# A second level of Strassen for three of the seven second-layer products, with their results added by an accumulating DMA

## The chip, the cores and the metric

The kernel runs on one core of a Trainium2 chip. The metric is the device time of one execution, in microseconds (us), as the median of several runs.

## The reference

A retention block feeds a feed-forward block. For each of 4 batches and 8 heads a state of 64 x 64 is carried over 768 positions, and its output is the input of two matrix products with a leaky ReLU between them:

```python
for t in range(S):
    state = gamma * state + einsum('bhd,bhe->bhde', k[:, :, t], v[:, :, t])
    y[:, :, t] = scale * einsum('bhd,bhde->bhe', q[:, :, t], state)
x = y.transpose(0, 2, 1, 3).reshape(B * S, H * D)     # 3072 tokens x 512
h = x @ w_in                                          # 512 x 2048
g = maximum(0.01 * h, h)
out = g @ w_out                                       # 2048 x 512
```

The weights come as float64 and are turned into float32 on the chip; all products are in float32.

## The kernel before

**Tiles.** The tokens are cut into six chunks c of 128 positions x 4 batches = 512 tokens. Activations lie with features on the partitions: x, g and o are tiles of 128 partitions x 4 blocks x 2 halves x 256 tokens. The hidden dimension is cut into four units u of 512. For each chunk and unit, the first layer multiplies a 512 x 512 piece of w_in by x, the leaky ReLU follows, and the second layer multiplies a 512 x 512 piece of w_out by g and adds the result to o.

**Strassen.** A 512 x 512 x 512 product is made by the Winograd form of Strassen: seven products M1 to M7 of 256-blocks from sums of blocks (`differences`, line 623, makes those of g in the tile gd and in g[1]). One such product is four matmuls of 128 x 128 weights by 256 columns (`seven`, line 641; its matmul is line 662). For chunks 2 to 5 the first layer goes one level further: each of its seven products is again made of seven products of 128-blocks, 49 in all. `inner` (line 1171) computes them in two groups, group 0 with 28 matmuls (M1, M4, M5 and M6 of the outer level) and group 1 with 21 (line 1184, 128 columns each); ScalarE and VectorE bring each bank to a tile `made`, and `outer` (line 1210) combines the seven results on VectorE (lines 1229 to 1239) and applies the leaky ReLU on ScalarE (line 1226). The weight sums for this are made once, kept in DRAM (`kept`), and streamed for each unit into the tiles wa and wb (`load_unit`, line 1054).

**The second layer** (`output`, line 735) takes seven products in the order FUSED: M1, M5, M6, M2, M7, M3, M4. Four PSUM rooms A, B, C, D (banks 5, 4, 7, 6) collect them: A holds M1 and then M1 + M2; ScalarE copies A to B after M1, so that B holds M1 + M6 and then also M7; C holds M5, then M5 + M3; D gets a copy of B and then M4. Each room is added to its block of o by VectorE (`plus`, line 606), or copied by ScalarE in the first unit of a chunk.

**Order.** The scheduling is manual: each engine does its instructions in the order in which the code writes them, and waits on semaphores only for data and for free buffers. The loop at line 1281 runs over 16 steps n, with c = 2 + n // 4 and u = n % 4. A step writes, in this order: the differences of g of unit n; group 0 of the first layer of unit n + 1; for u < 2 (and while a next chunk exists) a "visit", `joint_visit` (line 412), which reads the retention state for two batches of chunk c + 1 through banks 0, 1, 2 and 7; the second-layer products M1, M5, M6 of unit n; the scores of the next pair (`scores_of_pair`, line 356); M2; sums of the next x on VectorE (`differences` of x for u = 1, `sums_of_x` for u = 2); group 1 of the first layer of unit n + 1; M7; `outer`; M3 and M4. Banks 0 to 3 serve `inner`. In a visit, two memsets on GpSimd (`rows_free`, line 406) order groups of matmuls, and GpSimd then multiplies the next values by their decay (`decay_v`, line 158; its operation is line 161). All DMAs of this part are issued from SyncE (SP), one after another.

**Other names.** `new_g` (line 803) makes the tiles g and gd of a unit; `block(k, i)` (line 85) gives weight block i of half-unit k, where an even k = 2u belongs to the first layer and an odd one, 2u + 1, to the second; blocks 0 to 3 are the quarters, 4 to 6 the Strassen sums. `piece` (line 510) says where a loaded piece of weights goes. The line numbers are those of the kernel before.

## Time and profile before

| | us |
|---|---|
| median of three runs | 637.8 (637.6 to 638.4) |
| the profiled execution | 637.82 |
| its span, first to last instruction | 636.0 |
| TensorE busy in the span | 628.8 |
| VectorE busy | 464.1 |
| ScalarE busy | 268.9 |
| GpSimd busy | 23.3 |
| DMA: moved in all | 113.42 MB, 178 GB/s |

How to read it: the profile takes one execution. A group of instructions is one line of code, engine and operation with the tiles that it writes and reads, its count, its busy time and the mean duration of one, then the idle time of the engine ahead of it and what ended that. The fp32 matmul appears as two records. A duration in a group includes a part that overlaps with the next instruction, so that the distance from start to start is shorter. In the timelines, the first number is the start, the second the time until the last of the merged instructions ends; what stands in square brackets is the idle time before it and what released it. The chain of waits follows the execution back from its last instruction.

The stretches of the profile: chunks 0 and 1 up to about 224 us, the passage into the loop up to 252, then unit n = 0 (252 to 277), n = 1 to 3 (to 351), chunk 3 (n = 4 to 7, to 452), chunk 4 (n = 8 to 11, to 551), chunk 5 (n = 12 to 15).

### The profile page before, as it was taken

Reading aid. Unit: us, or ns where it says so; the run is one execution under the profiler, and the core shown is the slowest. Engines: PE = TensorE matmul, PEld = TensorE weight load, DVE = VectorE, ACT = ScalarE, POOL = GpSimd, SP = SyncE. Lnnn points to the kernel's source line nnn. Section 1 sums busy time; section 2 is a strip of 40 time slices with the busy share of each in tenths; the row PEclk is TensorE's granted clock in tenths of the full one; section 3 lists DMA queues with packets and bytes.
Section 4 is the critical chain, followed back from the end, with each engine's and each line's share of the span. In section 5 each row is a group of like instructions: output and inputs, shape, how many; then the busy total and the mean of one; then the engine's idle time right before and its main releaser. Section 6 shows DMA issues by size and latency. Waiting matters only on the chain.

```text
span 636.0 us, 14285 instructions
## 1 busy us (share of the span) xinstructions
PE 628.8 (99%) x6086; PEld 568.8 (89%) x6086; DVE 464.1 (73%) x760; ACT 268.9 (42%) x515; POOL 23.3 (4%) x45
## 2 busy tenths in 40 slices
PE   8999999999999999999999999999999999999997
PEld 5888888888888889899999999999999999999996
DVE  5679769889979986576785666877737768636655
ACT  4876556347343124242352442423433423534421
POOL 2000000000011010101000101000010000000000
PEclk9999999999999999999999999999999999999999
DMA  8941426556863998376735392864455236444201
GB/s 331 404 131 38 128 67 220 148 174 194 283 250 110 351 333 280 103 238 193 259 88 184 120 295 79 268 195 140 137 169 185 87 123 197 154 162 158 87 1 68
DMA packets 87537, 113.42 MB, mean 178 GB/s; under 512 B 3241, under 2 KB 71721, under 8 KB 87473
## 3 DMA queue, kind: packets, MB, share of 16 engines
q1 hardware_dynamic: 87168, 111.88, 53.2%
q8 instruction: 48, 0.79, 0.5%
q10 hardware_dynamic: 304, 0.62, 0.3%
q14 instruction: 17, 0.13, 0.1%
HBM read 93.35 MB, written 19.14 MB: 177 GB/s over the span
## 4 chain that ended last, share of the span: by engine, by line
PE 95%; DVE 2%; ACT 1%; DMA 1%; issue 0%; DVEq 0%; ACTq 0%
PE bank L662 32%; PE bank L1184 27%; PE C_h L662 4%; PE B_o L662 4%; PE A_h L662 4%; PE C_o L662 4%; PE A_o L662 4%; PE B_h L662 4%; PE D_h L662 2%; PE D_o L662 2%; PE d L683 2%; PE bank L369 1%; PE bank L444 1%; PE bank L427 1%; PE bank L380 1%; DMA t<-decay_dram 1%
## 5 line engine op out<-in xcount | busy, mean ns | idle before, releaser
L606 DVE TENSOR_TENSOR made<-made,bank 128x512 f32<-128x512 f32 (+1 forms) x96 | 56.4, 618 | 55.9 <-PE bank L1184 51.5
L606 DVE TENSOR_TENSOR o<-o,bank 128x512 f32<-128x512 f32 (+2 forms) x91 | 58.5, 661 | 51.8 <-PE bank L662 31.2
L662 PE MATMUL bank<-g,w 128*128 128x256 f32 x384 | 89.9, 382 | 0.0
L662 PEld LDWEIGHTS bank<-g,w 128*128 128x128 f32 x384 | 70.7, 190 | 9.2
L1184 PEld LDWEIGHTS bank<-x,wb 128*128 128x128 f32 x672 | 77.6, 192 | 0.8
L1184 PE MATMUL bank<-x,wb 128*128 128x128 f32 x672 | 77.6, 275 | 0.0
L1184 PE MATMUL bank<-x,wa 128*128 128x128 f32 x512 | 67.7, 275 | 0.0
L662 PE MATMUL bank<-gd,w 128*128 128x256 f32 x288 | 66.1, 379 | 0.0
L1184 PEld LDWEIGHTS bank<-x,wa 128*128 128x128 f32 x512 | 63.5, 192 | 1.1 <-ACT made L1194 0.2
L662 PEld LDWEIGHTS bank<-gd,w 128*128 128x128 f32 x288 | 54.7, 190 | 7.4
L1184 PE MATMUL bank<-t,wa 128*128 128x128 f32 x384 | 53.3, 275 | 0.0
L1226 ACT ACTIVATE g<-g 128x512 f32<-128x512 f32 x64 | 39.3, 631 | 30.8 <-DVE g L606 30.8
L1184 PEld LDWEIGHTS bank<-t,wa 128*128 128x128 f32 x384 | 48.0, 192 | 0.0
L1188 ACT COPY bank<-bank 128x512 f32<-128x512 f32 (+1 forms) x32 | 16.7, 520 | 67.8 <-PE bank L1184 67.5
L606 DVE TENSOR_TENSOR g<-made 128x512 f32<-128x512 f32 x64 | 42.7, 688 | 1.2
L755 ACT COPY bank<-bank 128x512 f32<-128x512 f32 x17 | 9.7, 570 | 71.2 <-PE bank L662 71.1
L609 DVE TENSOR_TENSOR gd<-g,gd 128x512 f32<-128x512 f32 x48 | 33.2, 692 | 5.4 <-ACT g L1226 0.5
L776 ACT COPY bank<-bank 128x512 f32<-128x512 f32 x16 | 9.1, 570 | 46.4 <-PE bank L662 46.4
L662 PE MATMUL bank<-g,last 128*128 128x256 f32 x120 | 28.3, 380 | 0.0
L662 PE MATMUL bank<-gd,last 128*128 128x256 f32 (+1 forms) x124 | 27.5, 373 | 0.0
L662 PE MATMUL A_h<-x,w 128*128 128x256 f32 x112 | 26.6, 380 | 0.0
L662 PEld LDWEIGHTS bank<-gd,last 128*128 128x128 f32 x124 | 22.8, 190 | 3.2 <-DVE gd L609 0.3
(223 smaller groups left out, 1030.1 us busy)
## 6 DMA issues: line engine op xcount, KB each, us to landing
wa<-kept SPq DMA_DIRECT2D x16, 1344.0 KB, 7.2
raw<-in_weights_dram SPq DMA_DIRECT2D x31, 512.0 KB, 4.4
wb<-kept SPq DMA_DIRECT2D x16, 896.0 KB, 5.7
wa<-kept SPq DMA_DIRECT2D x16, 448.0 KB, 4.4
wb<-kept SPq DMA_DIRECT2D x16, 448.0 KB, 6.3
out_dram<-o SPq DMA_DIRECT2D x23, 256.0 KB, 3.1
kept<-w SPq DMA_DIRECT2D x12, 448.0 KB, 6.0
qk<-in_qk_dram SPq DMA_DIRECT2D x10, 512.0 KB, 8.0
```

Source lines behind the costliest of these rows:

```text
L369: nc.tensor.matmul(at[j][ts(h, 64), n, m, i], lhsT=x[ts(j, 64), 1, a, ts(h, 64)], rhs=x[ts(j, 64), 0, a, ts(h, 64)], start=(n == 0 and a = ...
L380: nc.tensor.matmul(sums[h][ts(j, 64), n, a], lhsT=key[ts(h, 64), 2 * a + j], rhs=val[ts(h, 64), 2 * a + j], start=(n == 0 and a == 0), sto ...
L427: mm = nc.tensor.matmul(at[n][j][ts(i, 64), m, ts(h, 64)], lhsT=by_half[h][ts(j, 64), n, a], rhs=x[ts(j, 64), 0, a, ts(h, 64)], start=(n = ...
L606: nc.vector.tensor_tensor(out=out, in0=a, in1=b, op=ALU.add)
L609: nc.vector.tensor_tensor(out=out, in0=a, in1=b, op=ALU.subtract)
L662: nc.tensor.matmul(to, lhsT=block(w, sa)[:, k, ts(i, 128)], rhs=rhs[:, k, a:z], start=(first and (i == 0 or split) and n == 0 and k == 0), ...
L683: nc.tensor.matmul(banks[r][:, i, :], lhsT=block(2 * u, r + 2 * kh)[:, k, ts(i, 128)], rhs=x[:, 2 * kh + th, k, :], start=(step == 0 and i ...
L755: nc.scalar.copy(out=bank_of("B"), in_=ps)
L776: nc.scalar.copy(out=bank_of("D"), in_=ps)
L1184: nc.tensor.matmul(ps[q][:, i], lhsT=w[:, j, i], rhs=part_of(moving[i], s), start=(i == 0 and m in ("M1", "M5", "M4")), stop=True, skip_gr ...
L1188: nc.scalar.copy(out=ps[3], in_=ps[0])
L1226: nc.scalar.activation(g[:, i], g[:, i], AF.Prelu, alpha=0.01)
```

## The change

For units n = 4 to 14 (`by_leaves`: chunks 3, 4 and 5 without the very last unit) the second layer is split. The *trunk* computes M1, M5, M6 and M7 as before, without M2, M3 and M4, and without the copy to room D. The *leaves* compute M2, M3 and M4 by a second level: seven products of 128-blocks each, 21 matmuls of 128 columns in place of 12 of 256. They run through banks 6, 7, 2 and 5 after the trunk and after group 1 of the first layer.

- Their weight sums are made in chunk 2 on VectorE (`sums_of_rows`; u = 0 and 1 in step n = 0, u = 2 in n = 2, u = 3 in n = 3), stored to DRAM by 7 DMAs a unit (10 for u = 3), and loaded again for each unit by three DMAs from SP (`load_rows`).
- The sums of their moving operands are made by four subtractions a unit on GpSimd (`leaf_sums`), in units with a visit between the visit's memsets and the decay.
- Their results go to SBUF (`leaf_results`) by five copies on ScalarE and three additions on VectorE a unit. For u = 0, 1, 2 one accumulating DMA from GpSimd adds them to o[:, 0:3]; for u = 3 three additions on VectorE do, each followed by its store.
- What the trunk's rooms mean is spread in another way: A goes to o[0], B after M6 to o[1], B after M7 to o[2] and o[3], C to o[1] and o[3].
- The leaky calls of `outer` are deferred and written between the leaves' products.
- g and gd are one tile, with gd in reverse order, so that the operands of M2, M3 and M4 lie side by side; the weight blocks of odd half-units are placed anew for the same reason. The tiles that these blocks filled serve as leaf weights and scratch from chunk 3 on.

```diff
...
 
+    PLACE = {3: 4, 6: 3, 4: 6}
+
     def block(k, i):
...
         if k < N_UNITS - 1:
-            return unit(k)[:, i]
+            return unit(k)[:, PLACE.get(i, i) if k % 2 else i]
         return units[k][i // 2][:, i % 2] if i < 6 else last_s4[:, 0]
...
 
-    def joint_visit(c, b, banks=None):
+    def joint_visit(c, b, banks=None, behind=None):
 
...
             heads.pop((c, b + n))
+        if behind is not None:
+            behind()
         if later is not None:
...
 
+    PLACES = slice(2, 5, 2)
+
     def piece(n):
...
         if k < N_UNITS - 1:
+            if k % 2 and h:
+                return unit(k)[:, PLACES, i, :]
             return unit(k)[:, 2 * h : 2 * h + 2, i, :]
...
     slot = [0]
+    last_three = {}
+
+    class Reversed:
+
+        def __init__(self, tile):
+            self.tile = tile
+
+        def __getitem__(self, at):
+            return self.tile[:, 6 - at[1]]
 
...
         slot[0] = 1 - i
-        g = work.tile([128, 4, 2, N], FP32, tag=f"g{i}", name=f"g_{c}_{u}")
-        gd = work.tile([128, 3, 2, N], FP32, tag=f"gd{i}", name=f"gd_{c}_{u}")
-        return u, g, gd
+        both = work.tile([128, 7, 2, N], FP32, tag=f"g{i}", name=f"g_{c}_{u}")
+        last_three[c, u] = both[:, 2:5]
+        return u, both[:, 0:4], Reversed(both)
 
...
 
-    streamed = []
+    streamed, streamed_flat = [], []
     N2 = (NC - 2) * NU
...
         streamed.append(flat[:, 0 : 21 * C].rearrange("p (j i n) -> p j i n", j=7, i=3))
+        streamed_flat.append(flat)
 
...
         return block[:, k, ts(t, C)]
+
+    leaf_kept = [dram.tile([128, 3, 7, C], FP32, name=f"leaf_kept_{u}") for u in range(NU)]
+
+    def flat_of(part):
+        return part.rearrange("p i k n -> p (i k n)")
+
+    def leaf_rooms():
+
+        free = [flat_of(unit(k)[:, 2:5]) for k in (1, 3, 5)]
+        spare = [x2_place[0][:, 21 * C :], streamed_flat[0][:, 21 * C :]]
+        more = [spare[i // 2][:, ds(i % 2 * 3 * C, 3 * C)] for i in range(4)]
+        return free, spare, [x.rearrange("p (q n) -> p q n", q=3) for x in more]
+
+    def rows_of(u):
+
+        if u < NU - 1:
+            return [((0, 3, 1), unit(2 * u + 1)[:, 2:5])]
+        return [((0, 3, 2), units[2 * u + 1][1]), ((1, 2, 1), last_s4)]
+
+    def sums_of_rows(u):
+
+        free, _, more = leaf_rooms()
+        if u == NU - 1:
+            more = more[0:2] + [x[:, 7 * C : 10 * C].rearrange("p (q n) -> p q n", q=3)
+                                for x in free[0:2]]
+        bases = [[] for _ in range(3)]
+        for at, blocks in rows_of(u):
+            which = slice(*at)
+            a11, a21, a12, a22 = (blocks[:, :, k, ts(m, C)] for k in range(2) for m in range(2))
+            r = [x[:, which] for x in more]
+            plus(r[0], a21, a22)
+            minus(r[1], r[0], a11)
+            minus(r[2], a12, r[1])
+            minus(r[3], a11, a21)
+            for base, a in zip(bases, (a11, a12, a22)):
+                base.append((which, a))
+
+        def keep():
+            for j, parts in enumerate(bases):
+                for which, a in parts:
+                    nc.sync.dma_start(out=leaf_kept[u][:, which, j], in_=a)
+            for j, r in enumerate(more):
+                nc.sync.dma_start(out=leaf_kept[u][:, :, 3 + j], in_=r)
+        return keep
+
+    def load_rows(n):
+
+        free, spare, _ = leaf_rooms()
+        leaf_weights[:] = [x[:, 0 : 7 * C].rearrange("p (j n) -> p j n", j=7)
+                           for x in (free[0], free[1], spare[1])]
+        for to, kept_rows in zip(leaf_weights, (leaf_kept[at_of(n)[1]][:, i] for i in range(3))):
+            nc.sync.dma_start(out=to, in_=kept_rows)
+
+    leaf_weights = []
+
+    def by_leaves(n):
+        return n >= NU and n < N2 - 1
+
+    def leaf_sums(n):
+
+        free, spare, _ = leaf_rooms()
+        made = [x.rearrange("p (q n) -> p q n", q=3)
+                for x in (free[0][:, 7 * C : 10 * C], free[1][:, 7 * C : 10 * C],
+                          spare[0][:, 0 : 3 * C])]
+        three = last_three[at_of(n)]
+        b11, b12, b21, b22 = (three[:, :, k, ts(h, C)] for k in range(2) for h in range(2))
+        for out, a, b in ((made[0], b12, b11), (made[1], b22, made[0]), (made[2], b21, made[1]),
+                          (b12, b22, b12)):
+            nc.gpsimd.tensor_tensor(out=out, in0=a, in1=b, op=ALU.subtract)
+        return [b11, b21, *made, b22, b12]
+
+    def leaf_steps(n, moving):
+
+        ps = [bank[i][:, 0 : 3 * C].rearrange("p (i n) -> p i n", i=3) for i in (6, 7, 2, 5)]
+        results = leaf_results()
+        for m, q, j, s in INNER:
+            for i in range(3):
+                nc.tensor.matmul(ps[q][:, i], lhsT=leaf_weights[i][:, j], rhs=moving[s][:, i],
+                                 start=(i == 0 and m in ("M1", "M5", "M4")), stop=True,
+                                 skip_group_check=True)
+            if m == "M1":
+                nc.scalar.copy(out=ps[3], in_=ps[0])
+            elif m == "M3":
+                plus(results[:, :, 1], results[:, :, 1], ps[1])
+            elif m == "M7":
+                plus(results[:, :, 3], results[:, :, 3], ps[3])
+                plus(results[:, :, 2], results[:, :, 2], ps[3])
+            else:
+                nc.scalar.copy(out=results[:, :, {"M5": 3, "M4": 2, "M6": 1, "M2": 0}[m]],
+                               in_=ps[q])
+            yield
+
+    def leaf_results():
+        return flat_of(unit(5)[:, 2:5]).rearrange("p (i q n) -> p i q n", i=3, q=4)
+
+    def leaf_results_taken(c, o, final):
+
+        results = leaf_results()
+        if not final:
+            nc.gpsimd.dma_start(out=o[:, 0:3].rearrange("p i k n -> p (i k n)"),
+                                in_=results.rearrange("p i q n -> p (i q n)"), accum_op=ALU.add)
+            return
+        for i in range(3):
+            plus(o[:, i], o[:, i], results[:, i].rearrange("p (k h) n -> p k (h n)", k=2))
+            nc.sync.dma_start(out=out[c, i], in_=o[:, i])
+
+    def trunk(c, o, part, first, final):
+
+        u, g, gd = part
+        ps = {x: room[x] for x in "ABC"}
+        for m, x, sa, rhs, start in (("M1", "A", 0, g[:, 0], True), ("M5", "C", 4, gd[:, 0], True),
+                                     ("M6", "B", 5, gd[:, 1], False),
+                                     ("M7", "B", 1, g[:, 1], False)):
+            for i in range(2):
+                for k in range(2):
+                    nc.tensor.matmul(ps[x][:, i, :], lhsT=block(2 * u + 1, sa)[:, k, ts(i, 128)],
+                                     rhs=rhs[:, k, :], start=(start and i == 0 and k == 0),
+                                     stop=(k == 1), skip_group_check=True)
+            if m == "M1":
+                nc.scalar.copy(out=ps["B"], in_=ps["A"])
+            elif m == "M6":
+                if first:
+                    nc.scalar.copy(out=o[:, 1], in_=ps["B"])
+                else:
+                    plus(o[:, 1], o[:, 1], ps["B"])
+            elif m == "M7":
+                yield
+                if first:
+                    nc.scalar.copy(out=o[:, 2], in_=ps["B"])
+                    plus(o[:, 3], o[:, 3], ps["B"])
+                else:
+                    plus(o[:, 2:4], o[:, 2:4],
+                         ps["B"].unsqueeze(1).to_broadcast([128, 2, 2, N]))
+                if final:
+                    nc.sync.dma_start(out=out[c, 3], in_=o[:, 3])
+            yield
+
+    def trunk_taken(o, first):
+
+        if first:
+            nc.scalar.copy(out=o[:, 0], in_=room["A"])
+            nc.scalar.copy(out=o[:, 3], in_=room["C"])
+            plus(o[:, 1], o[:, 1], room["C"])
+        else:
+            plus(o[:, 0], o[:, 0], room["A"])
+            plus(o[:, 1:4:2], o[:, 1:4:2],
+                 room["C"].unsqueeze(1).to_broadcast([128, 2, 2, N]))
 
...
 
-    held = []
+    held, keep_rows = [], []
     for n in range(N2):
...
             differences(*gs[n][1:])
+        if n == 0:
+            keep_rows.append(sums_of_rows(0))
         if n + 1 < N2 and u == NU - 1:
...
             xs[c + 1] = new_x(c + 1)
+        moving = []
+
+        def sums_for_leaves():
+            if by_leaves(n):
+                moving.extend(leaf_sums(n))
+
         if visiting:
-            joint_visit(c + 1, 2 * u)
-        steps = output(c, os[c], [gs.pop(n)], u == 0, u == NU - 1, room=room if more else last_room,
-                       order=FUSED if more else LAST, held=held if more else None)
+            joint_visit(c + 1, 2 * u, behind=sums_for_leaves)
+        else:
+            sums_for_leaves()
+        scores_next = visiting and following(c + 1, 2 * u)
+        part = gs.pop(n)
+        if by_leaves(n):
+            steps = trunk(c, os[c], part, u == 0, u == NU - 1)
+        else:
+            steps = output(c, os[c], [part], u == 0, u == NU - 1, room=room if more else last_room,
+                           order=FUSED if more else LAST, held=held if more else None)
         products(steps, 3)
-        if c + 1 < NC and u < 2 and following(c + 1, 2 * u):
-            scores_of_pair(*following(c + 1, 2 * u))
+        if scores_next:
+            scores_of_pair(*scores_next)
         if visiting:
             load_unit(n + 2, 0)
-        products(steps, 1)
+        while keep_rows:
+            keep_rows.pop(0)()
+        if by_leaves(n):
+            if visiting and u > 0:
+                products(steps, 2)
+            trunk_taken(os[c], u == 0)
+            if visiting and u == 0:
+                products(steps, 2)
+        else:
+            products(steps, 1)
         if c + 1 < NC and u == 1:
...
             sums_of_x(c + 1, 0)
+        if c == 2 and u != 1:
+            keep_rows.append(sums_of_rows({0: 1, 2: 2, 3: 3}[u]))
         if more:
...
                 ahead(c + 2, 2 * u + i)
+            while keep_rows:
+                keep_rows.pop(0)()
             products(steps, 1)
-            outer(n + 1, 1)
+            later = [] if by_leaves(n) else None
+            outer(n + 1, 1, later)
+        if by_leaves(n):
+            products(steps, 1)
+            leaves = leaf_steps(n, moving)
+            for count in (2, 1, 1, 1) if visiting else (1, 3, 1, 0):
+                if not visiting:
+                    later.pop(0)()
+                products(leaves, count)
+                if visiting:
+                    later.pop(0)()
+            products(leaves, 8)
+            leaf_results_taken(c, os[c], u == NU - 1)
+        if more and by_leaves(n + 1):
+            load_rows(n + 1)
         if n + 2 == N2:
...
     nc = bacc.Bacc("TRN2", target_bir_lowering=False, num_devices=1,
-                   dynamic_dma_scratch_size=256)
+                   dynamic_dma_scratch_size=512)
     arrays, args = {}, []
...
```

## The prediction

> **What bounds the kernel now.** I read the page's engine shares first, then the busy time by stretch, the chain of waits, and last the timelines of single units. A unit n (0 to 15) is one pass of the loop at line 1281: c = 2 + n // 4, u = n % 4.
>
> ```profile
> span 636.0 us, 14285 instructions
> PE 628.8 (99%) x6086; PEld 568.8 (89%) x6086; DVE 464.1 (73%) x760; ACT 268.9 (42%) x515; POOL 23.3 (4%) x45
> ```
> TensorE is never idle for long. The stretches of units 5 and 6 (columns: length; busy PE, PEld, DVE, ACT, POOL; clock; DMA share, GB/s):
>
> ```profile
> 378.39:406.05 27.66, 27.66 (x381) 25.58 (x380) 19.78 (x34) 10.31 (x21) 2.24 (x4) 1.00 0.60 194
> 406.05:429.08 23.03, 23.03 (x156) 21.58 (x156) 17.61 (x32) 8.74 (x16) 0.00 (x0) 1.00 0.58 190
> ```
> From unit 1 to unit 14 every stretch has PE busy for its whole length. So less PE work shortens the kernel one for one, and any new PE wait lengthens it one for one. Unit 6 in the chain (start, us, what; two records a matmul):
>
> ```profile
> 406.05 6.25 PE bank L1184 x56
> 412.30 6.91 PE bank L662 x32
> 419.21 4.69 PE bank L1184 x42
> 423.89 5.18 PE bank L662 x24
> ```
> These are the 28 first-layer matmuls of group 0, four second-layer products (1.73 us each), the 21 of group 1, and the last three products, 5.18 us. That last row also shows that 21 matmuls of 128 columns cost 4.69 us where 12 of 256 cost 5.18.
>
> [...] POOL's v<-v,dec takes 1104 ns on average, 1.02 where two stand undisturbed (2.04 at 390.43)[...].
>
> **Removed and added on PE.** Units 4 to 14, eleven of them, replace 5.18 by 4.69 us: 11 x 0.49 = **-5.4 us**. Leaf matmuls have the shape of those of line 1184, so I take their rate.
>
> **Rows that I price with** (busy, mean ns):
>
> ```profile
> L606 DVE TENSOR_TENSOR made<-made,bank 128x384 f32<-128x384 f32 x48 | 25.2, 552 | 44.8 <-PE bank L1184 44.0
> L1226 ACT ACTIVATE g<-g 128x512 f32<-128x512 f32 x64 | 39.3, 631 | 30.8 <-DVE g L606 30.8
> L1194 ACT COPY made<-bank 128x384 f32<-128x384 f32 x16 | 7.7, 478 | 3.9 <-PE bank L1184 3.9
> L161 POOL TENSOR_TENSOR v<-v,dec 128x512 f32<-128x512 f32 x14 | 15.2, 1104 | 33.1 <-DMA v<-in_kv_dram 14.8 <-DVE x L609 9.5 <-PE bank L662 8.7
> ```
> In sequence VectorE starts a 512-wide op every 0.60 us (403.84, 404.44, 405.04), so a 384-wide one every 0.47 and a 1024-wide one every 1.15; a result of PE is taken 0.2 us after its end.
>
> **Weight sums of the rows, chunk 2.** Four 384-wide VectorE ops for each u, 0.55 us each with dependences: 2.15 us; u = 3 about 3.0. Those of u = 1, 2, 3 stand ahead of L606 made in units 0, 2, 3, where VectorE idles for 3 to 4 us or where the three products that still follow on PE (5.18 us) cover the lag: 0. Those of u = 0 stand between the differences and the made ops of unit 0:
>
> ```profile
> 254.99 0.68 DVE L609 TENSOR_TENSOR g<-g 128x512 f32<-128x512 f32 x1
> 255.59 1.88 DVE L606 TENSOR_TENSOR made<-made,bank 128x512 f32<-128x512 f32 x3
> 256.33 0.69 PE L427 MATMUL bank<-qk,states 64*64 64x64 f32 x32 [0.18 <-DVE made L606]
> ```
> VectorE has no gap here, and PE already waits for made: the visit's read writes bank 1, which M3's add must have emptied. So 2.15 us goes straight onto PE: **+2.15**. The seven stores for each u cost SP some 0.5 us each, 3.6 us; behind them in unit 0 is the wb load at 272.0, and SP is free from 267.6: 0. Their 1344 KB each use idle DMA share (0.59): 0.
>
> **The end of a leaf unit.** Let T0 be the end of the 21 matmuls of group 1. In before, three products (5.18 us) cover VectorE's adds of line 1210 and ScalarE's four leaky. Now leaves stand there, and ScalarE's queue mixes their copies with the leaky calls, so a leaf product can wait, through a copy, for a leaky, and so for VectorE. With visit (u = 0, 1): PE does a leaf product every 0.67 us, and M7 (start T0 + 4.02) needs bank 5 back from the copy of M6. ScalarE's order is copies M1, M5, leaky 0, copy M4, leaky 1, copy M6. If VectorE is on time, made ends at T0 + 1.2, leaky 0 runs 1.97 to 2.6, M4 to 3.0, leaky 1 to 3.6, M6 to 4.03: a wait of 0.1. **+0.2** for units 4 and 8. VectorE isn't on time where x's sums stand ahead of made. Unit 5 before:
>
> ```profile
> 396.82 0.69 DVE L609 TENSOR_TENSOR t<-x 128x512 f32<-128x512 f32 x1
> 400.30 1.62 DVE L606 TENSOR_TENSOR made<-made,bank 128x384 f32<-128x384 f32 x3 [0.74 <-PE bank L1184]
> ```
> The gap is 0.74 us. Now the take of trunk M7 (1024 wide, 1.15) and that of bank C (1024, 1.15 where A's 0.60 stood alone) come first. Counted from M6's end: o1 to 0.8, masks and state to 3.0, M7's take 4.05 to 5.2, A to 5.8, C to 6.95, four differences (2.88) to 9.8, while M3 is ready at 8.13. The lag of 1.7 passes to leaky 0 and the copy of M6: PE waits **+1.5** in unit 5. Unit 9 likewise, **+1.5**, and as chunk 5 has no later scores, its M7 follows M6 at once and waits for o1's add as well: 0.2 + 0.69 = **+0.9**. Units 6 and 10 (u = 2) carry 3.26 us of sums of x (419.85 to 423.11), a lag of 1.5; their M7 stands ahead of the leaves, leaky 0 ahead of copy M1, and leaf M6 waits for that copy: 7.92 + 0.63 + 0.46 = 9.0 against 8.43, **+0.6** each. Units 7, 11 and 12 to 14 have no such sums ahead of made: 0. In sum the leaf ends cost 0.2 + 1.5 + 2.4 + 1.2 = **+5.3**.
>
> **GpSimd.** Four 384-wide subtractions a unit, by 1.02 x 384/512 about 0.8 each, 3.3 us after the differences; leaves come over 12 us later. In units with a visit they stand ahead of decay_v, whose values the scores need: decay ends 392.47, read from 393.09, so 0.6 us of slack, and v lands only at 390.4. From the visit's last memset (386.24) the sums end at 389.5, or 391 if they collide with two VectorE ops. Between 0 and 1 us in units 4, 5, 8; I take **+0.4** together.
>
> **Accumulating DMA**, nine of 768 KB (u = 0 to 2). [...] Results are whole 1.2 us after the leaves' end L; the next add to o is due at L + 6.25 + 5.18 + 0.2 = L + 11.6, a window of 10.4 us, 12.6 with a visit. I take 0 there. A VectorE stopped by it would hold trunk, x's sums and made behind it. On POOL, behind the issue, are the next visit's memsets, due at L + 6.6: covered. After unit 14 the window is shorter: PE goes on into unit 15's products, whose M7 needs o1 added by L + 8.5, so the DMA ended by 7.7, 6.5 after its release: [...] I take **+0.5**. Weight loads (three SP issues a unit) are due a whole unit later: 0. Unit 7 and 11 add 3 x 0.60 on VectorE ahead of the differences, which end at L + 6.1, before the trunk's M5: 0.
>
> **Sum.** -5.4 + 2.15 + 5.3 + 0.4 + 0.5 = +3.0. The profiled execution took 637.82 us, 636.0 of span and 1.8 around it; the median of three runs is 637.8. Forecast **640.8**.
>
> **Rivals.** *No lag* (chance 0.19): VectorE's lag ahead of made in units 5, 6, 9, 10 is worth 4.2 us and exists only if the two 1024-wide takes really cost 1.15 and the sums of x stay ahead. If it is under 0.1 (visit) or 0.9 us (u = 2), copies come in time, and 640.8 - 4.2 = 636.6, without the tail's and GpSimd's allowance 635.7: faster. The 0.74 us gap speaks against it. *Slow accumulation* (0.28): the DMA's add runs at a fraction of a copy's rate. From 10.4 us on it stops VectorE at o1 and then PE: at 14 us some 3.5 in units 6 and 10, 1.5 in 5, 7, 9, 11, and 6 at the tail, about 19, so 660; at 11.5 some 9, so 650. The low DMA share (0.40 to 0.60) speaks against it, the missing row leaves it open. *The lag as worked out* has 0.53, 638 to 644.
>
> **How the numbers follow.** About 0.2% (1.3 us) is what a measurement can tell from no change. Faster than 636.5: the first rival's larger part, 0.17. Within: its rest and the lower edge of the forecast, 0.17. Slower 0.66. The range 635 to 655 leaves out the slowest accumulations and a little below.
>
> **What would show it.** Leaf products in 4.69 us; in unit 0 PE waiting 2 us for made; in 5 and 9 leaf M7 waiting for a copy, 1.5; no VectorE wait for the DMA in units 5 to 14. A wait of o's adds for the DMA, or leaves without waits, would make it wrong.

## The result and the profile after

The changed kernel takes 658.8 us (median of four runs, 657.0 to 660.3) against 637.9 for the kernel before on the same chip: a ratio of 1.0326, interval 1.0298 to 1.0353. The forecast was 640.8. The profiled execution took 658.26 us with a span of 656.4, so 20.4 us more span than before. Line numbers are from here on those of the changed kernel; up to line 1078 most have moved by 4 to 10 (L606 is now L614, L662 L670), the first-layer matmul is L1349, the trunk's L1300 and the leaves' L1262.

The head of the page:

```profile
span 656.4 us, 15061 instructions
PE 631.5 (96%) x6284; PEld 574.3 (87%) x6284; DVE 501.5 (76%) x803; ACT 283.5 (43%) x559; POOL 82.3 (13%) x98
```

PE is busy 2.7 us longer although it has less to do, and idle 24.9 us where it was idle 7.2: the loss is in waits, and in work done at a lower clock. The stretches of unit 1 (which still has no leaves), in the kernel before and in this one, and of units 5 and 6 in this one (length; busy PE, PEld, DVE, ACT, POOL; clock; DMA share, GB/s):

```profile
277.39:304.87 27.48, 27.48 (x412) 25.50 (x412) 20.46 (x35) 10.28 (x21) 2.24 (x4) 1.00 0.61 200
279.77:317.34 37.57, 31.43 (x412) 28.96 (x412) 26.69 (x46) 11.55 (x23) 2.24 (x4) 0.86 0.69 220
393.90:423.91 30.01, 27.83 (x399) 25.79 (x398) 22.92 (x36) 11.56 (x26) 7.81 (x9) 1.00 0.84 265
423.91:447.32 23.41, 22.80 (x174) 21.79 (x174) 18.59 (x33) 10.38 (x21) 5.17 (x5) 1.00 0.87 275
```

Unit 1 took 27.48 us before, so half of the whole loss lies in a unit that was forecast to cost nothing. What the chain of waits shows of the leaves themselves is as forecast: 21 leaf matmuls in 4.69 us.

```profile
561.11 4.69 PE bank L1349 x42
565.79 1.73 PE bank L1300 x8
567.52 4.69 PE bank L1262 x42
```

Three groups take longer than in the kernel before, or than the forecast took them: `made` out of SBUF alone (688 ns before), a 384-wide sum of x (552 before), and GpSimd's subtractions, taken at 800.

```profile
L614 DVE TENSOR_TENSOR made<-made 128x512 f32<-128x512 f32 x32 | 25.4, 794 | 1.7
L1253 POOL TENSOR_TENSOR w<-g,w 128x384 f32<-128x384 f32 x11 | 12.7, 1153 | 0.9
L617 DVE TENSOR_TENSOR x<-x 128x384 f32<-128x384 f32 x8 | 7.6, 951 | 0.0
```

### The profile page after: what moved, and what is told of

Read it like the earlier page. It is cut to its first block, busy times and chain, and to the rows that moved or that the text cites. A ratio compares the mean times of both kernels' runs of the same rounds, so it can differ in the third digit from the quotient of the medians.

```text
span 656.4 us, 15061 instructions
## 1 busy us (share of the span) xinstructions
PE 631.5 (96%) x6284; PEld 574.3 (87%) x6284; DVE 501.5 (76%) x803; ACT 283.5 (43%) x559; POOL 82.3 (13%) x98
## 5 line engine op out<-in xcount | busy, mean ns | idle before, releaser
L614 DVE TENSOR_TENSOR o<-o,bank 128x512 f32<-128x512 f32 (+3 forms) x75 | 55.4, 768 | 38.8 <-PE bank L1300 12.9
L614 DVE TENSOR_TENSOR made<-made,bank 128x512 f32<-128x512 f32 (+1 forms) x96 | 55.5, 616 | 33.5 <-PE bank L1349 29.9
L1349 PEld LDWEIGHTS bank<-x,wb 128*128 128x128 f32 x672 | 77.6, 192 | 1.1 <-ACT bank L1353 0.3
L1349 PE MATMUL bank<-x,wb 128*128 128x128 f32 x672 | 77.9, 275 | 0.1
L1349 PE MATMUL bank<-x,wa 128*128 128x128 f32 x512 | 70.4, 282 | 6.2 <-DVE made L614 3.2
L1349 PEld LDWEIGHTS bank<-x,wa 128*128 128x128 f32 x512 | 65.1, 198 | 7.2 <-DVE made L614 3.4
L1300 PE MATMUL bank<-g,w 128*128 128x256 f32 x288 | 67.0, 383 | 3.7 <-DVE x L468 2.9
L617 DVE TENSOR_TENSOR g<-g 128x512 f32<-128x512 f32 x96 | 64.1, 688 | 5.6 <-ACT g L1391 0.5
L1300 PEld LDWEIGHTS bank<-g,w 128*128 128x128 f32 x288 | 53.0, 190 | 12.5 <-DVE x L468 4.5
L1349 PE MATMUL bank<-t,wa 128*128 128x128 f32 x384 | 54.6, 280 | 0.0
L1349 PEld LDWEIGHTS bank<-t,wa 128*128 128x128 f32 x384 | 49.3, 196 | 0.0
L614 DVE TENSOR_TENSOR g<-made 128x512 f32<-128x512 f32 x64 | 45.9, 738 | 3.1
L670 PE MATMUL bank<-g,w 128*128 128x256 f32 x168 | 38.0, 382 | 0.0
L670 PEld LDWEIGHTS bank<-g,w 128*128 128x128 f32 x168 | 31.3, 190 | 4.2
L670 PE MATMUL bank<-g,last 128*128 128x256 f32 (+1 forms) x148 | 32.6, 375 | 0.0
L670 PEld LDWEIGHTS bank<-g,last 128*128 128x128 f32 x148 | 27.0, 190 | 3.9 <-DVE g L617 0.4
L1262 PE MATMUL bank<-g,w 128*128 128x128 f32 x176 | 27.2, 277 | 2.4 <-ACT w L1273 2.4
L614 DVE TENSOR_TENSOR made<-made 128x512 f32<-128x512 f32 x32 | 25.4, 794 | 1.7
L670 PE MATMUL A_h<-x,w 128*128 128x256 f32 x112 | 26.6, 380 | 0.0
L1262 PEld LDWEIGHTS bank<-g,w 128*128 128x128 f32 x176 | 23.7, 192 | 3.2 <-issue 1.4
```

Of the source, the lines that this page charges most:

```text
L614: nc.vector.tensor_tensor(out=out, in0=a, in1=b, op=ALU.add)
L617: nc.vector.tensor_tensor(out=out, in0=a, in1=b, op=ALU.subtract)
L670: nc.tensor.matmul(to, lhsT=block(w, sa)[:, k, ts(i, 128)], rhs=rhs[:, k, a:z], start=(first and (i == 0 or split) and n == 0 and k == 0), ...
L1262: nc.tensor.matmul(ps[q][:, i], lhsT=leaf_weights[i][:, j], rhs=moving[s][:, i], start=(i == 0 and m in ("M1", "M5", "M4")), stop=True, sk ...
L1300: nc.tensor.matmul(ps[x][:, i, :], lhsT=block(2 * u + 1, sa)[:, k, ts(i, 128)], rhs=rhs[:, k, :], start=(start and i == 0 and k == 0), sto ...
L1349: nc.tensor.matmul(ps[q][:, i], lhsT=w[:, j, i], rhs=part_of(moving[i], s), start=(i == 0 and m in ("M1", "M5", "M4")), stop=True, skip_gr ...
```

## Where the 20 us are

I took the length of every unit (from the start of its first-layer group 0 to the next) in both traces, and every wait that the timeline of PE labels. Units 7 and 11, where no new wait stands, are 0.49 us shorter than before, the gain that was forecast.

| unit | before | after | labelled PE waits that are new |
|---|---|---|---|
| 0 | 28.17 | 30.30 | 2.30 for `made` |
| 1 | 27.48 | 37.57 | 3.23 for `made`, 2.92 for a bank |
| 4 | 27.47 | 30.44 | 0.79 for x (L468), 1.57 + 0.31 for v |
| 5 | 27.65 | 30.00 | 0.70 for x, 0.32 for v, 1.17 of a leaf |
| 6, 10 | 23.03 | 23.41 | 0.60 of a leaf, in each |
| 7, 11 | 23.03 | 22.54 | none |
| 8 | 27.47 | 28.09 | 0.69 for x |
| 9 | 25.25 | 28.32 | 0.70 for x, 0.83 for o, 1.26 of a leaf |

Unit 6 has a wait of 0.60 and is 0.87 longer than unit 7, so this short wait costs some 0.27 more than its label. With that the rows of the table from unit 4 on close within 0.2: unit 5, for example, should be 27.65 - 0.49 + 2.19 + 3 x 0.27 = 30.16, and is 30.00.

**Unit 1.** The VectorE timeline of unit 1 and SP's of units 0 and 1, in the kernel after:

```profile
281.10 0.56 DVE L614 TENSOR_TENSOR x<-w 128x384 f32<-128x384 f32 x1 [11.33 <-DMA leaf_kept<-x]
283.28 1.47 DVE L614 TENSOR_TENSOR made<-made,bank 128x384 f32<-128x384 f32 x3
```

```profile
269.72 3.14 SPq L1225 DMA_DIRECT2D leaf_kept<-w  x3
272.96 3.38 SPq L1227 DMA_DIRECT2D leaf_kept<-x  x2
276.43 2.78 SPq L1227 DMA_DIRECT2D leaf_kept<-wb  x2
```

The weight sums of u = 1 write the same scratch that those of u = 0 wrote, and the stores of u = 0 have not yet read it: SP issues them only at 269.7 to 279.2, behind two wa loads, 1.4 us each. The store that VectorE's first operation waits for (leaf_kept<-x) is the fourth of them: issued at 272.96, done when the wait ends at 281.10. So some 3.2 of the 11.33 us that VectorE stands still pass before that store is issued, and 8.1 until it has landed. The `made` operations of unit 1 are queued behind, and PE waits for these; the second wait passes through ScalarE, whose copy stands behind the leaky calls that came late with VectorE. In the PE timeline:

```profile
283.88 2.89 PE L1349 MATMUL bank<-x,wa 128*128 128x128 f32 x16 [3.23 <-DVE made L614]
289.69 2.50 PE L1349 MATMUL bank<-x,wa 128*128 128x128 f32 x10 [2.92 <-ACT bank L1353]
```

These waits are 6.2 of unit 1's 10.1 us. The rest is the clock, in the stretches around them (clock third from the end):

```profile
284.00:285.00 1.00, 1.00 (x9) 1.00 (x10) 1.00 (x3) 0.00 (x0) 0.00 (x0) 0.94 1.07 325
290.00:292.00 2.00, 2.00 (x11) 2.00 (x11) 1.77 (x3) 1.12 (x3) 0.00 (x0) 0.50 1.14 342
296.00:297.00 1.00, 1.00 (x65) 0.96 (x68) 0.85 (x2) 0.00 (x0) 0.10 (x1) 1.00 0.00 0
```

From 284.9 to 295.1 it is 0.50, in the trace's clock records for 10.24 us. Apart from the second wait, 7.3 us of work ran at half speed, which costs 3.7: 6.2 + 3.7 = 9.9 of the 10.1.

**Units 4, 5, 8, 9: GpSimd beside VectorE.** Unit 4, GpSimd's subtractions and VectorE in one timeline:

```profile
371.10 1.00 POOL L1253 TENSOR_TENSOR w<-g 128x384 f32<-128x384 f32 x1
371.14 1.51 DVE L614 TENSOR_TENSOR made<-made 128x512 f32<-128x512 f32 x1
372.18 1.32 POOL L1253 TENSOR_TENSOR w<-g,w 128x384 f32<-128x384 f32 x1
372.68 1.37 DVE L614 TENSOR_TENSOR g<-made 128x512 f32<-128x512 f32 x1
373.58 1.33 POOL L1253 TENSOR_TENSOR x<-g,w 128x384 f32<-128x384 f32 x1
373.98 1.41 DVE L468 TENSOR_TENSOR x<-bank,dec 128x256 f32<-128x256 f32 x4
```

Two VectorE operations between tiles in SBUF take 1.51 and 1.37 us instead of 0.69 while GpSimd's subtractions run beside them; two of the subtractions take longer too, 1.32 and 1.33 instead of 1.00. Behind them stand the visit's takes (L468), which empty bank 7, into which the trunk's M5 wants to go. The forecast charged the collision to the decay alone.

**Units 4, 5: the load of v.** The decay waits for v, which SP issued at 371.83 and which is there at 379.7, after 7.9 us; in the kernel before it was issued at 359.29 and there at 363.06 (first line), after 3.8. The 1344 KB of leaf weights, issued at 368.4 to 369.9, and two stores of o stand right ahead of it.

```profile
363.06 2.04 POOL L161 TENSOR_TENSOR v<-v,dec 128x512 f32<-128x512 f32 x2 [4.54 <-DMA v<-in_kv_dram]
379.73 2.04 POOL L163 TENSOR_TENSOR v<-v,dec 128x512 f32<-128x512 f32 x2 [3.86 <-DMA v<-in_kv_dram]
380.83 0.69 PE L382 MATMUL bank<-v,k 64*64 64x64 f32 x32 [1.57 <-POOL v L163]
```

**The accumulating DMA** ends none of these waits; that it delays v in unit 5 comes out of an experiment below. Its row (KB, median us from issue to landing; the single ones lie between 5.8 and 10.8), and the only wait for it in the list of waits, one of VectorE after unit 14:

```profile
o<-w POOLq DMA_DIRECT2D x9, 768.0 KB, 8.9
```

```profile
DVE o L614 <- DMA o<-w: 3.0, 1, 3.0
```

## The experiments

Theory A: the loss is a sum of four costs, namely the weight sums in chunk 2 (12.3 us, 10 of them from reused scratch), GpSimd's subtractions in VectorE's way (about 4), v's load behind the leaf weights (about 3) and the leaf ends as forecast (about 6). Theory B: the leaves themselves, their accumulating DMA above all, are what is slow. All medians are against 637.9 for the kernel before.

**Chunk 2 alone.** The sums and stores stay, no unit goes by leaves. This kernel leaves the leaves out, and the scratch of the last sums overwrites weights that its plain second layer still reads, so its output is not the reference's.

```diff
-        return n >= NU and n < N2 - 1
+        return False
```

> Keeps the weight sums of the leaf rows in chunk 2 and their stores, and computes every second-layer product of chunks 3 to 5 as before the change: no leaves, no GpSimd subtractions, no accumulating DMA, no leaf weight loads. Theory A (unit 0 of chunk 2 makes TensorE wait for VectorE, first for the sums of u = 0, then because the sums of u = 1 wait for the stores of those of u = 0 out of the same scratch; 12.4 us of the 20.4 us): 650.3 us, with TensorE at half clock for some 8 us after the second wait. Theory B (the leaf units with their DMAs cost most of it): below 641 us.

651.4 us, ratio 1.0204 (1.0184 to 1.0224). The three waits stand where they stand in the changed kernel (here 2.30, 2.34 and 3.75 us), and units 4 to 13 have their old lengths within 0.02 us. The clock behaves otherwise than expected: one stretch of 3.4 us at half rate behind the first wait and one around the end of the last, not some 8 us behind the second. Some 13 us of the loss come from chunk 2 with no leaf in the program, which B does not allow.

**One set of sums a unit**, all of them in the later place, ahead of the first layer's group 1, so that the scratch has been read:

```diff
-        if n == 0:
-            keep_rows.append(sums_of_rows(0))
...
-        if c == 2 and u != 1:
-            keep_rows.append(sums_of_rows({0: 1, 2: 2, 3: 3}[u]))
+        if c == 2:
+            keep_rows.append(sums_of_rows(u))
```

> The whole change, but the sums of u are made in unit n = u of chunk 2, each in the later of the two places (ahead of the first layer's group 1), so that none stands ahead of unit 0's made and none follows another within a unit. Theory A: both waits of unit 0 go, 658.8 - 12.4 = 646.4 us, TensorE's clock full. Theory B: about 657 us.

647.4 us, ratio 1.0141 (1.0126 to 1.0156). Units 0 and 1 take 28.18 and 27.47 us, as before: the sums and their stores are all still there, and cost nothing measurable in units 0 to 3, where they stand now.

**Only the second set moved**, u = 0 stays ahead of unit 0's `made`:

```diff
-        if c == 2 and u != 1:
-            keep_rows.append(sums_of_rows({0: 1, 2: 2, 3: 3}[u]))
+        if c == 2 and u > 0:
+            keep_rows.append(sums_of_rows(u))
```

> The whole change, with only the sums of u = 1 moved, from unit 0 to unit 1; the sums of u = 0 stay ahead of unit 0's made. Theory A: only the second wait goes, 658.8 - 10.1 = 648.7 us, with a wait of 2.3 us left in unit 0. If the first wait were the one that drops the clock: 654 us or more.

647.8 us, ratio 1.016 (1.013 to 1.0191). Unit 0 keeps its 2.3 us (30.43), unit 1 is back at 27.47. So of the 12.3 us, 2.2 are the term that was forecast (2.15), and 10.1 come from the reuse of the scratch. Against the experiment before, the medians do not show the 2.3 us; the profiles do in unit 0, and this one's unit 4 is 3.2 us shorter: there the other waits 2.29 + 0.31 for v, with a stretch at a clock of 0.50 behind, from 370.8 to 374.0 or later, and this one 0.78 for x and 0.31 for v.

**Subtractions behind the decay** (on top of one set a unit):

```diff
-            joint_visit(c + 1, 2 * u, behind=sums_for_leaves)
-        else:
-            sums_for_leaves()
+            joint_visit(c + 1, 2 * u)
+        sums_for_leaves()
```

> As the kernel with one sum a unit, and in units with a visit GpSimd's four subtractions stand behind the two decay operations instead of ahead of them. Theory A (the subtractions collide with VectorE's adds ahead of the visit's results, and trunk M5 waits for those): the waits of M5 for the visit's results go in units 4, 5, 8, 9, 0.9 us each, so 646.4 - 3.6 = 642.8 us. If the waits for the decayed values come from GpSimd's order too, up to 2.5 us more, 640.3; if they come from the load of the values, nothing more. Theory C (the added 1024-wide VectorE operations make M5 wait): no change, 646.4 us.

643.7 us, ratio 1.0089 (1.0068 to 1.0109). M5's wait for x is gone in units 5 and 8 and stays in unit 9 (0.69), where no decay stands ahead of the subtractions and so nothing moved. In unit 4 the kernel that this one builds on has no such wait. There the first VectorE operation beside GpSimd's subtractions began 0.03 us ahead, and GpSimd's took longer, not VectorE's:

```profile
359.07 0.69 DVE L614 TENSOR_TENSOR made<-made 128x512 f32<-128x512 f32 x1
359.10 1.52 POOL L1253 TENSOR_TENSOR w<-g 128x384 f32<-128x384 f32 x1
```

The waits for v remain (1.76 + 0.30 and 0.52 + 0.32), although no subtraction stands ahead of the decay on GpSimd now: the load is late. The 3.7 us between the two medians are not the price of the collision. In the profiles 2.4 of them lie in unit 4, where v came sooner and the clock did not fall (1.00 from 364 to 372 us); unit 8 gives 0.8; and in unit 5, no shorter than before, PE now waits for v where it waited for x.

**Leaf weights loaded behind v** (on top of the last one): `load_rows` moves from the end of the unit before to the place behind the visit.

```diff
+        if by_leaves(n):
+            load_rows(n)
...
-        if more and by_leaves(n + 1):
-            load_rows(n + 1)
```

> As the kernel with the subtractions behind the decay, and the three DMAs for leaf weights are issued behind the visit of the same unit, not at the end of the unit before. Theory A (the values for the decay come late since the DMA engines are still full of leaf weights): the waits for the decayed values in units 4 and 5 (2.1 and 0.8 us) go, 640.6 us. If the stores of the sums and the accumulating DMA hold the values up: less than 1 us gained. If the weights come late for the leaves: slower, and leaf M1 waits for a DMA.

641.2 us, ratio 1.0055 (1.004 to 1.007), so 2.5 us less by one move of three DMA issues. The same two lines of this kernel's timeline show v there in time, without a wait of PE:

```profile
363.75 2.04 POOL L163 TENSOR_TENSOR v<-v,dec 128x512 f32<-128x512 f32 x2 [5.10 <-DMA v<-in_kv_dram]
365.61 1.11 PE L382 MATMUL bank<-v,k 64*64 64x64 f32 x64
```

In units without a visit the loads now come late: leaves wait for weights 0.68, 0.39 and 0.45 us in units 6, 10 and 13.

**Sums of the next x moved to the next unit**, away from the leaf ends of units 5 and 9 (on top of the subtractions behind the decay):

```diff
+        if u == 2 and c + 1 < NC and by_leaves(n - 1):
+            differences(*xs[c + 1])
...
-        if c + 1 < NC and u == 1:
+        if c + 1 < NC and u == 1 and not by_leaves(n):
```

> As the kernel with the subtractions behind the decay (643.7 us), and in units 5 and 9 the four differences of the next x, which stand ahead of VectorE's adds for the first layer, are made in the unit after, behind the differences of g. Theory A (VectorE's lag reaches leaf M7 through ScalarE's queue of leaky calls and copies): the waits for the copy in units 5 and 9 (1.25 each[...]) go, 640.8 us, and no new one comes. Theory C (ScalarE itself is too slow among the leaves): the waits stay, 643.7 us.

645.6 us, ratio 1.0113 (1.0095 to 1.0132): a miss by some 5 us. The leaf waits of units 5 and 9 went, which confirms the forecast's reason for them. But in units 6 and 10 the wait rose from 0.60 to 1.84, since the moved operations now run beside GpSimd's subtractions (a later experiment takes them apart, and these waits go):

```profile
416.01 1.30 POOL L1253 TENSOR_TENSOR w<-g 128x384 f32<-128x384 f32 x1 [0.84 <-DVE g L617]
416.38 1.49 DVE L617 TENSOR_TENSOR t<-x 128x512 f32<-128x512 f32 x1
417.40 1.32 POOL L1253 TENSOR_TENSOR w<-g,w 128x384 f32<-128x384 f32 x1
417.90 1.37 DVE L617 TENSOR_TENSOR t<-x,t 128x512 f32<-128x512 f32 x1
```

The trace has two half-clock stretches besides, of 3.4 us each at 0.50, behind the waits for v in units 4 and 5 (1.67 + 0.31 and 1.11 + 0.32), which are 1.5 and 0.9 us longer than in the experiment that this one builds on.

**No accumulating DMA**: VectorE adds all leaf results (on top of the subtractions behind the decay).

```diff
-        if not final:
-            nc.gpsimd.dma_start(out=o[:, 0:3].rearrange("p i k n -> p (i k n)"),
-                                in_=results.rearrange("p i q n -> p (i q n)"), accum_op=ALU.add)
-            return
...
+            if not final:
+                continue
```

> As the kernel with the subtractions behind the decay, but the leaf results of u = 0, 1, 2 are added to o by three VectorE additions of 512 elements, as for u = 3, and no DMA accumulates. Theory A (the accumulating DMA is hidden, apart from 3 us that VectorE waits at the tail with little effect): between 643 and 645.5 us, since 1.8 us of VectorE a unit come in a place where nothing waits. Theory B (the accumulating DMA costs in its units): 640 us or less.

648.6 us, ratio 1.0167 (1.0152 to 1.0182), 4.9 more than with the DMA. Both theories missed here: A put the adds at little, B wanted a gain. The end of the kernel loses most: unit 14 and what follows take 42.48 us instead of 38.93, for VectorE's adds now stand ahead of the last unit's differences, and PE waits for those, with a half-clock stretch of 3.4 us behind the wait:

```profile
PE bank L670 <- DVE g L617: 2.0, 1, 2.0
```

Unit 4, where no accumulating DMA has run yet, is 1.7 longer, with a half-clock stretch of 3.4 us behind its wait for v. Unit 5 gains 1.25 us, for its wait for v is gone: from issue to the decay v takes 3.7 us here and 5.8 in the kernel that this one builds on. With the accumulating DMA but without the leaf weights just ahead (the experiment with these behind v) it takes 3.6. So in unit 5 the two together make v late, and the forecast's 0 for the DMA is not quite right. On balance the DMA earns its place, and theory B falls.

**All of it together**: the three moves, the leaky calls of units without a visit in the order of the others (behind the leaves' products, not ahead), and M7 of unit 9 behind o's add.

```diff
-            if visiting and u > 0:
+            if visiting and u > 0 and scores_next:
...
-            for count in (2, 1, 1, 1) if visiting else (1, 3, 1, 0):
-                if not visiting:
-                    later.pop(0)()
+            for count in (2, 1, 1, 1):
                 products(leaves, count)
-                if visiting:
-                    later.pop(0)()
+                later.pop(0)()
```

> The subtractions behind the decay, the next x's differences a unit later, the leaf weights behind the visit, the copies of leaf M1 and M5 ahead of the first leaky call in all leaf units, and in unit 9, which has no scores, trunk M7 behind the first layer's group 1. Theory A: of 643.7 go 2.9, 3.1, 1.6 (units 6 and 10) and 1.0: 635.1 us, faster than the kernel before, with a wait of 0.7 us left for the visit's results in unit 9. Theory B: some wait takes the place of those removed, 638 us or more.

637.6 us, ratio 0.9995 (0.9986 to 1.0003): as fast as the kernel before, 2.5 us short of what was expected. What is left stands in units 6 and 10 (0.9 and 1.0 us over the units behind them: the collision with GpSimd), 9 (the wait for x, 0.70) and 13 (leaf weights, late by 0.37).

**The collision and the late weights mended**: the sums of x stand ahead of g's differences, so ahead of the subtractions, and only units with a visit load late.

```diff
+            if u == 2 and c + 1 < NC and by_leaves(n - 1):
+                differences(*xs[c + 1])
             differences(*gs[n][1:])
...
-        if by_leaves(n):
+        if by_leaves(n) and visiting:
             load_rows(n)
```

> As the kernel with all edits (637.6 us), with two more: in units 6 and 10 the next x's differences stand ahead of those of g, so that GpSimd's subtractions, which wait for g's, don't run beside them; and only units with a visit get their leaf weights late, the others at the end of the unit before. Theory A (in units 6 and 10 each VectorE difference lost some 0.75 us to a GpSimd subtraction, and the lag became a TensorE wait; in unit 13 the leaf weights came late): 0.6 each in units 6 and 10, 0.65 in 13 and 0.2 in 7 and 10 go, 635.6 us. If the lag of units 6 and 10 has another cause: 636.8 us.

635.1 us, ratio 0.9958 (0.9945 to 0.9972): faster than the kernel before. One labelled wait of PE is left from unit 1 on, 0.70 for x in unit 9.

**The same with the subtractions on VectorE:**

```diff
-            nc.gpsimd.tensor_tensor(out=out, in0=a, in1=b, op=ALU.subtract)
+            minus(out, a, b)
```

> The kernel before this one, with the four subtractions for the leaves on VectorE in place of GpSimd, at the same place in the order: behind the visit's results, or ahead of the trunk. Theory A (GpSimd's subtractions cost more VectorE time by collision than VectorE needs to do them itself): unit 9's wait for the visit's results (0.7[...]) goes and no other comes, 634.7 us, 0.5% faster than the kernel before the change. Theory C (VectorE has no 2.2 us a unit left): leaf or trunk waits grow, 637 us or more.

633.8 us, ratio 0.9936 (0.9923 to 0.9948), the best version, 25 us below the changed kernel. Its page and the stretch of unit 6:

```profile
span 631.2 us, 15016 instructions
PE 624.4 (99%) x6284; PEld 570.8 (90%) x6284; DVE 511.6 (81%) x847; ACT 283.7 (45%) x559; POOL 31.3 (5%) x54
```

```profile
404.90:427.54 22.64, 22.64 (x174) 21.79 (x174) 21.88 (x40) 10.21 (x22) 0.90 (x1) 1.00 0.97 301
```

PE has no labelled wait over 0.25 us in the loop, and its busy time is 4.4 us below that of the kernel before. Unit 9 is 0.98 us shorter than in the kernel that this one builds on. The expectation's reason, that the collision takes more VectorE time than the subtractions, does not hold: VectorE's busy time rose from 496.9 to 511.6 us. What was gained is the wait. VectorE is busy for 21.9 of unit 6's 22.6 us, so there is no more room in that unit.

**That edit alone** (on top of one set of sums a unit, without the other moves):

> As the kernel with one sum a unit (647.4 us), only with the four subtractions on VectorE in place of GpSimd. Theory A (the collision with GpSimd delays VectorE's adds ahead of the visit's results): trunk M5's waits for them go in all four units 4, 5, 8 and 9, in unit 9 too, where the order of GpSimd's work alone could not remove it: 643.8 us or a little less. Theory C (those waits come from VectorE's added work): they stay or grow, 647 us or more.

643.5 us, ratio 1.0084 (1.007 to 1.0098), 3.9 less than the same kernel with GpSimd. M5's waits for x, 0.70 each in units 5, 8 and 9 of that kernel, are all gone, in unit 9 too, where moving the subtractions had changed nothing; the leaf waits (1.11, 0.54, 1.10, 0.55) stay. So the waits for x came from GpSimd's subtractions and from nothing else in that place. They are worth 1.0 and 1.1 us in units 8 and 9. The rest of the 3.9 is v's: unit 4 is 2.4 us shorter, with waits of 1.82 + 0.30 and no half-clock stretch (mean granted clock of the execution 0.999; with GpSimd 0.996), and unit 5 is 0.7 longer, with waits of 1.23 + 0.32 for v that the other did not have.

## Why the prediction was wrong

The forecast had the sign, faintly, and missed the size: +3.0 against +20.4 us of span. By its own terms (from the waits of the profile, from unit 4 on each counted as its label plus 0.27; the last row is the remainder):

| term | forecast | after | shown by |
|---|---|---|---|
| products, 11 x 0.49 | -5.4 | -5.4 | units 7, 11; leaves 4.69 |
| weight sums of u = 0 | +2.15 | +2.1 | only the second set moved |
| weight sums of u = 1, 2, 3 | 0 | +10.1 | one set a unit; only the second set moved |
| leaf ends | +5.3 | +5.8 | sums of x moved; waits of 0.60 to 1.26 |
| GpSimd's subtractions | +0.4 | +4.0 | subtractions on VectorE: 1.0 a wait in units 8, 9 |
| weight loads | 0 | +3.0 | leaf weights loaded behind v |
| DMA, tail, small rest | +0.5 | +0.8 | no experiment |

**The step that failed** is "Those of u = 1, 2, 3 stand ahead of L606 made in units 0, 2, 3, where VectorE idles for 3 to 4 us ... : 0". The room for four operations was there; the experiment with one set a unit uses just such room and pays nothing. What I did not ask is what the first of them must wait for. It writes scratch whose reader is a DMA that had not even been issued, and that took 8.1 us from issue to the end of the wait. The same paragraph followed these seven stores through SP, priced them (at 0.5 us each; they took some 1.4 each, with two wa loads just ahead) and asked only whom they would delay on SP, not who waits for them to have read. Nor did it see a wait as more than its length: the clock stood at 0.50 for 10.24 us behind it, worth another 3.7 us. Both sit in one term, and it is half of the result.

**GpSimd.** The forecast named the collision ("if they collide with two VectorE ops") and counted its cost on GpSimd's side only: later subtractions, later decay. The mis-sized term is VectorE's side. It holds the visit's takes and through bank 7 the trunk: four waits, 2.88 us by label. The duration was low as well: a subtraction of 384 takes 0.99 us at the shortest, not 0.8, and 1.15 in the mean.

**Weight loads.** The term "due a whole unit later: 0" was right for the leaf weights and silent on those behind them. v has little slack (0.6 us, which the forecast itself worked out), and it queued behind 1344 KB: 7.9 us from issue to arrival in unit 4, where it took 3.8 before.

**What held.** The PE gain; the price of the first sums; the leaf ends, in place and nearly in size, against the rival that saw no lag there (units 5 and 9: 1.17 and 1.26 where 1.5 was forecast, 0.83 for 0.9, 0.60 for 0.6; units 4 and 8 none for 0.1); and the accumulating DMA, which ends inside its window, though it helps to delay v in unit 5. The rival of a slow accumulation forecast 650 to 660 us and would have met the time by accident; its mechanism is refuted, since the one wait for that DMA comes in the tail, and removing the DMA made that part longer. What such a DMA takes, and so the 0 for it in the units and the 0.5 us for the tail, were the author's estimates, for the kernel before issues none. Measured, its 768 KB take 5.8 to 10.8 us from issue to landing. How its rate compares with that of a plain copy was not shown: no run copies the same bytes in the same place.

What stays open: how much of the spread of the changed kernel (3.2 us over four runs) is the clock. The mean granted clocks of the four runs go with their times: 0.995 at 657.0 us, 0.992 at 658.3, 0.987 at 659.4 and 660.3. From 0.995 to 0.987 of 656 us are some 5 us of full-rate work, an estimate from these figures that covers the whole spread; where the clock fell in the other three runs is not on record. Half-clock stretches also differ between the experiments, so differences of a few us between their medians are not prices of one wait.

## What to carry to other kernels

Before calling an engine's extra work covered by its idle time, ask what its first instruction waits for, the readers of the scratch that it overwrites included; a store that another engine has still to issue, or that has not landed, is such a reader. Here it held VectorE for 11.33 us, and PE waited 3.23 and 2.92 us for what stood behind. Put loads into a queue by the slack of what stands behind them, not by their own: here moving three loads behind that of v gained 2.5 us. On a kernel bound by PE a change that saves half a microsecond a unit is worth only what its waits leave: here the same change, 20.9 us slower as made, became 4.1 us faster than the kernel before once its new waits were moved away and the subtractions stood on VectorE.

## What the runs showed of the hardware

- Ahead of the last instructions of a kernel, the granted clock fell to 0.50 for single stretches: for 10.24 us in the changed kernel, for about 3.4 us each time in the experiments on chunk 2 alone (from 259.64 and 290.36), with the sums of x moved (368.48 and 399.20) and without the accumulating DMA (368.76 and 631.58), and for at least 3.2 us with one set of sums a unit (370.78). Each of these began in a wait of PE or up to 2.1 us behind one; the waits were of 1.11 to 3.75 us. Not every wait of this size had one: none followed the 1.76 us in unit 4 with the subtractions behind the decay. The wait of 2.30 us in unit 0 was followed by one in the experiment on chunk 2 alone (first line, clock third from the end) and by none in the changed kernel (second line). What decides between the two cases was not shown.

```profile
260.00:261.00 1.00, 1.00 (x48) 1.00 (x46) 0.90 (x2) 0.00 (x0) 0.10 (x1) 0.50 0.08 16
260.00:261.00 1.00, 1.00 (x42) 0.91 (x34) 0.97 (x2) 0.00 (x0) 0.00 (x0) 1.00 0.08 16
```

- In the stretches shown above, VectorE operations of 512 elements between tiles in SBUF took 1.37 to 1.51 us beside a GpSimd subtraction, where `made` out of SBUF takes 0.69 in the kernel before, and GpSimd's subtractions 1.30 to 1.52 us instead of 1.00. In the two pairs that began almost together, the second to begin took longer: in unit 4 of the changed kernel GpSimd began 0.04 us ahead and took 1.00, VectorE 1.51; with one set of sums a unit VectorE began 0.03 us ahead and took 0.69, GpSimd 1.52.
- A wait of PE for another engine cost 0.27 and 0.28 us beyond its label in two places: a wait of 0.60 cost 0.87 in unit 6 of the changed kernel, and one of 0.70 cost 0.98 in unit 9 before the subtractions went to VectorE.
- One SP issue of a weight store took 0.5 to 1.4 us in unit 3 and 1.0 to 1.8 in unit 0, there with two wa loads of together 1792 KB just ahead; a load of v that took 3.8 us in the kernel before took 7.9 in the changed kernel behind 1344 KB and two stores of o.
